# A first FFN block cut into two halves of 128 tokens, whose pieces are held back until their weights are rounded

## The chip, the core and the metric

The kernel runs on one core of a Trainium2 chip. Its engines work side by side, each through its own list of instructions in order: TensorE (PE in the profile, with its weight loads as PEld), VectorE (DVE), ScalarE (ACT), GpSimd (POOL) and SyncE (SP), which issues most of the DMAs. The metric is the device time of one execution in microseconds; the median of four runs of the kernel before is 1777.9 us (1777.15 to 1778.71).

## What is computed

```python
# attention: q, k, v of shape (8, 8, 576, 64)
scores = scale * np.matmul(q, k.transpose(0, 1, 3, 2))
kth = np.partition(scores, -32, axis=-1)[..., -32:-31]
scores = np.where(scores >= kth, scores, -1000000000.0)
attn = np.exp(scores - np.max(scores, axis=-1, keepdims=True))
attn = attn / (np.sum(attn, axis=-1, keepdims=True) + 1e-09)
o = np.matmul(attn, v)
# bridge: (B,H,S,D) -> (B*S, H*D), 4608 tokens of 512
x = o.transpose(0, 2, 1, 3).reshape(B * S, H * D)
# FFN: w_gate, w_val 512 x 1536, w_out 1536 x 512
g = x @ w_gate
out = (g * (1.0 / (1.0 + np.exp(-g))) * (x @ w_val)) @ w_out
```

## The kernel before

**Units.** Attention is cut into 160 units. A unit is one batch, one tile of 128 queries and one pair of heads; units run in the order batch, query tile, head pair, so four units make all 512 features of 128 tokens. The last query tile of each batch (`qt == J`, units 16 to 19 of the first batch) has 64 queries for both heads together and costs half. The main loop `for n in range(NU + 3)` (L747) writes for unit n, in this order: the scores of the units after it (`scores`, PE L306 or L292, scaled on ACT L311), the attention-times-v products of units n-4 and n-3 (`values`, PE L421, copied into `xT` on ACT L437), the exponentials of unit n-1 (`weigh`, ACT L353 and L358), the top-k of unit n (`select`, DVE L326 and L330), the transposes of unit n-2 (`turn`, PE L387), the normalizing of unit n-1 (`normalize`, DVE L369 and L370, then POOL L373). Scores and values are written in even units only, for two units at a time.

**FFN blocks.** The FFN takes 256 tokens at a time (`BLK`), 18 blocks. `feed(kb)` (L459 on) is a generator. For each of six steps s it multiplies the transposed tokens `xT` by two 128-column slices of `w_gate` and of `w_val` (PE L477, 128x256 moving), evacuates them with three ACT instructions for the gate (L502 to L504) and one for the value (L509), and multiplies on POOL (L505, L510) into a tile `h`. Then comes the product with `w_out`: twelve matmuls of 128x512 for each 128 tokens in block 0 (L523, the `plain` form), and seven quarter products (L563) in every later block. A `yield` ends a piece: in the first part four 128x256 matmuls, in the plain part two 128x512 matmuls. Each is one credit; three quarter matmuls are 0.75.

**Credit.** `share(n)` gives every unit a number of credits, 7 (later 6.4) less what its attention costs, and `pieces` spends them at four places of the unit. `piece()` starts the next block only when `done[kb]` says that all its tokens are in `xT`; without that it returns 0 and the credit is lost.

**Weights.** The three weight matrices are rounded on the chip while attention runs, in 36 pieces: `w_gate` and `w_val` in 24, in the order of the steps s, then twelve rows of `w_out`. Each piece is a DMA of 512 KB into one of three `w` buffers (L104), three ACT instructions (L112, L114, L115), one on DVE (L119) and two on POOL (L120, L121), the last of which frees the buffer. `rounding` and `early` place them among the instructions of the unit, some two and a half pieces in a unit; `ready[0]` counts those whose last step is written. In `feed`, `need(n)` writes roundings at once until n pieces are ready. After block 0, `weights` goes on to form sums of parts of `w_out` (L169 to L188) for the later blocks; a part of these waits for `plain_done`, which block 0 sets with its last product.

**Order.** Every engine keeps the order in which the code writes (the last loop of the function adds that dependency), so a waiting instruction holds what is written behind it on its engine.

Of the kernel before, what the change touches and what calls it, by code (L numbers as in the profile page):

```python
# [8 lines left out]
AF = mybir.ActivationFunctionType  # L9
ALU = mybir.AluOpType  # L10
FP32 = mybir.dt.float32
# [4 lines left out]
P = 128  # L16
# [4 lines left out]
BLK = 256  # L21
# [4 lines left out]
def kernel(  # L26
# [37 lines left out]
    nc = tc.nc  # L64
    B, H, S, D = q.shape
    DM, DFF = w_gate.shape
# [3 lines left out]
    NHP = H // 2  # L70
    KC = DM // P
    MC = DFF // P
    MS = MC // 2
    MQ = MC // 2
    NBLK = B * S // BLK
    scale = 1.0 / float(D) ** 0.5
# [8 lines left out]
    ffn = ctx.enter_context(tc.tile_pool(name="ffn", bufs=2))  # L85
    ps_t = ctx.enter_context(tc.tile_pool(name="ps_t", bufs=5, space=PSUM))
    ps_f = ctx.enter_context(tc.tile_pool(name="ps_f", bufs=3, space=PSUM))
# [9 lines left out]
    wg = consts.tile([P, KC, DFF], FP32, name="wg")  # L97
    wv = consts.tile([P, KC, DFF], FP32, name="wv")
    wo = consts.tile([P, MC, DM], FP32, name="wo")
# [93 lines left out]
    ready = [0]  # L193
    early = [lambda: None]
    plain_done = []
# [7 lines left out]
    def need(n):  # L203

        while ready[0] < n:
            next(weight)

    pairs = [(b, hp) for b in range(B) for hp in range(NHP)]
    raw, preps = {}, {}
# [186 lines left out]
    xT, done = {}, {}  # L396
# [47 lines left out]
    def store(o, g0, cols=slice(0, DM), queues=(nc.sync,)):  # L444

        at = g0
        while at < g0 + P:
            b, c = divmod(at, S)
            j, p0 = divmod(c, P)
            n = min(g0 + P - at, S - c, P - p0)  # L450
            r0 = b * S + (c if j == J else J * p0 + j)
            dst = out[r0 : r0 + n, :] if j == J else out[r0 : r0 + J * (n - 1) + 1 : J, :]
            queues[0].dma_start(dst[:, cols], o[at - g0 : at - g0 + n, cols])
            queues = queues[1:] + queues[:1]
            at += n

    on_act, on_pool = [], []

    def flush(queue):  # L459
        while queue:  # L460
            queue.pop(0)()

    def feed(kb):


# [2 lines left out]
        x = xT.pop(kb)  # L468
        hs = []

        def product(w, s, then):
            ps = ps_f.tile([P, 2, BLK], FP32, tag="f", name="f")
            need(4 * s + (2 if w is wg else 4))
            for i in range(2):
                m = 2 * s + i
                for kc in range(KC):
                    nc.tensor.matmul(  # L477
                        ps[:, i, :],
                        w[:, kc, m * P : (m + 1) * P],
                        x[:, kc, :],  # L480
                        start=(kc == 0),
                        stop=(kc == KC - 1),
                    )
                if i == 1:
                    on_act.append(lambda: then(ps))
                yield 1

        plain = kb == 0
        first, late = slice(0, P), slice(P, BLK)

        s32 = x[:].rearrange("p a b -> p (a b)")[:, 0 : MQ * P].rearrange(
# [3 lines left out]
        for s in range(MS):  # L495
            h = ffn.tile([P, 2, BLK], FP32, tag="h", name="h", bufs=MS + 1)
# [15 lines left out]
            yield from product(wg, s, gate)  # L512
            yield from product(wv, s, value)
        o = ffn.tile([P, 2, DM], FP32, tag="o", name="o", bufs=1)
        if plain:
            for t in range(2):
                ps = ps_f.tile([P, DM], FP32, tag="f", name="o_ps")
                for m in range(MC):
                    need(4 * MS + m + 1)
                    if m == 6:  # L520
                        flush(on_act)
                        flush(on_pool)
                    nc.tensor.matmul(  # L523
                        ps[:],
                        hs[m // 2][:, m % 2, t * P : (t + 1) * P],
                        wo[:, m, :],
                        start=(m == 0),
                        stop=(m == MC - 1),
                    )
                    if m == MC - 1:  # L530

                        def finish(ps=ps, t=t):
                            nc.scalar.copy(o[:, t, :], ps[:])
                            store(o[:, t, :], kb * BLK + t * P)

                        on_act.append(finish)
                        if t == 1:
                            plain_done.append(True)
                    if m % 2 == 1:
                        yield 1  # L540
            return
        while len(T[3]) < MQ:
            next(weight)
        DH = DM // 2
# [76 lines left out]
        if kb == NBLK - 1:  # L621
# [7 lines left out]
            for i, t, cols in ((4, 1, left), (3, 0, right)):  # L629
                ps = ps_f.tile([P, DH], FP32, tag="f", name="x_ps")  # L630
# [30 lines left out]
        on_act.append(rest_x)  # L661

    NU = len(units)
    todo = list(range(NBLK))
    current = []

    def piece():

        if len(on_act) > 1:
            flush(on_act)  # L670
        if len(on_pool) > 1:
            flush(on_pool)
        while True:
            if not current:
                if not todo or done.get(todo[0], 0) < NHP * BLK:
                    return 0
                flush(on_act)
                flush(on_pool)
                current.append(feed(todo.pop(0)))
            cost = next(current[0], 0)  # L680
            if cost == 0:
                current.pop()
                continue
            return cost
# [34 lines left out]
    def pieces(n):  # L719
        for _ in range(n):  # L720
            if credit[0] >= 1:
                credit[0] -= piece()
# [85 lines left out]
    while piece():  # L808
        pass
# [48 lines left out]
```

## Time and profile before

| | us |
|---|---|
| median of 4 runs | 1777.9 |
| profiled execution | 1779.02 |
| its span in the profile | 1777.2 |
| PE busy | 1679.6 (95%) |
| DVE busy | 1483.7 (83%) |
| ACT busy | 1163.4 (65%) |
| POOL busy | 959.3 (54%) |

The shares are means over stages that differ. Up to about 131 us the weights are rounded beside attention and no FFN block has begun; DVE works without a gap and PE is busy about half of the time. From there to the end PE is nearly always busy. DVE ends its last unit about 110 us before the end; what remains is FFN work of the last blocks. The start of a unit can be read on DVE: its first MAX8 reads `sc`, later ones read `e`. In the profile a fp32 matmul appears as two records of PE, so "x8" of L477 is four matmuls, one piece.

### The profile page before, as it was taken

Reading aid. Unit: us, or ns where it says so; the run is one execution under the profiler, and the core shown is the slowest. Engines: PE = TensorE matmul, PEld = TensorE weight load, DVE = VectorE, ACT = ScalarE, POOL = GpSimd, SP = SyncE. Lnnn points to the kernel's source line nnn. Section 1 sums busy time; section 2 is a strip of 40 time slices with the busy share of each in tenths; the row PEclk is TensorE's granted clock in tenths of the full one; section 3 lists DMA queues with packets and bytes.
Section 4 is the critical chain, followed back from the end, with each engine's and each line's share of the span. In section 5 each row is a group of like instructions: output and inputs, shape, how many; then the busy total and the mean of one; then the engine's idle time right before and its main releaser. Section 6 shows DMA issues by size and latency. Waiting matters only on the chain.

```text
span 1777.2 us, 31074 instructions
## 1 busy us (share of the span) xinstructions
PE 1679.6 (95%) x11012; PEld 1386.4 (78%) x11012; DVE 1483.7 (83%) x3371; ACT 1163.4 (65%) x2721; POOL 959.3 (54%) x1058
## 2 busy tenths in 40 slices
PE   5559999899999999999999999999999999999999
PEld 3337678688888878888888878887888878787887
DVE  6999888998999899998998888898988888888300
ACT  7788676676667576767666676666666666575521
POOL 3778655445464636464646445554445544646444
PEclk6669999899999999999999999999999999999999
DMA  7442030002100030002100020000300020000000
GB/s 194 129 119 84 21 87 1 13 1 62 35 5 9 15 82 2 13 1 51 47 13 1 13 71 26 1 13 17 80 1 13 1 56 14 13 1 13 1 13 12
DMA packets 109307, 59.68 MB, mean 34 GB/s; under 512 B 88544, under 2 KB 96992, under 8 KB 109152
## 3 DMA queue, kind: packets, MB, share of 16 engines
q1 hardware_dynamic: 108016, 57.37, 12.4%
q8 instruction: 87, 1.43, 0.3%
q14 instruction: 68, 0.56, 0.1%
q10 hardware_dynamic: 1136, 0.33, 0.1%
HBM read 48.23 MB, written 9.44 MB: 32 GB/s over the span
## 4 chain that ended last, share of the span: by engine, by line
PE 78%; POOL 8%; ACT 6%; DVE 4%; issue 3%; DMA 1%; SPq 0%; POOLq 0%; ACTq 0%; DVEq 0%
PE f L477 38%; PE av L421 10%; PE x_ps L563 8%; PE s L306 7%; PE etps L387 6%; PE y_ps L563 6%; POOL e L373 2%; ACT e L358 2%; DVE e L330 2%; DVE m L326 2%; PE s L292 2%; PE kqps L261 1%; PE o_ps L523 1%; ACT e L353 1%; POOL size L120 1%
## 5 line engine op out<-in xcount | busy, mean ns | idle before, releaser
L326 DVE MAX8 m<-e 128x8 f32<-128x576 f32 x864 | 615.5, 749 | 3.3
L330 DVE MATCH_REPLACE8 e<-m,e 128x576 f32<-128x576 f32 x576 | 424.1, 743 | 0.0
L477 PE MATMUL f<-xT,wg 128*128 128x256 f32 x1728 | 401.2, 381 | 0.0
L477 PE MATMUL f<-xT,wv 128*128 128x256 f32 x1728 | 399.7, 380 | 0.3 <-ACT half_g L503 0.3
L373 POOL TENSOR_TENSOR e<-e,tot 128x576 f32<-128x576 f32 x288 | 325.0, 1147 | 120.9 <-DVE tot L370 106.5
L477 PEld LDWEIGHTS f<-xT,wg 128*128 128x128 f32 x1728 | 323.3, 190 | 50.5 <-issue 8.5
L477 PEld LDWEIGHTS f<-xT,wv 128*128 128x128 f32 x1728 | 322.9, 190 | 49.7 <-issue 7.9
L505 POOL TENSOR_TENSOR h<-h,half_g 128x512 f32<-128x512 f32 x108 | 137.8, 1276 | 294.9 <-ACT h L504 291.6
L358 ACT ACTIVATE e<-e,bias 128x576 f32<-128x576 f32 x288 | 220.4, 768 | 75.6 <-POOL bias L341 73.2
L510 POOL TENSOR_TENSOR h<-h,val 128x512 f32<-128x512 f32 x108 | 137.7, 1275 | 184.8 <-ACT val L509 161.9
L387 PE MATMUL etps<-ident,e 128*128 128x128 f32 (+1 forms) x1312 | 184.3, 282 | 49.7 <-POOL e L373 29.2
L387 PEld LDWEIGHTS etps<-ident,e 128*128 128x128 f32 (+1 forms) x1312 | 154.4, 143 | 83.9 <-POOL e L373 39.2
L353 ACT ACTIVATE e<-sc,m 128x576 f32<-128x576 f32 x288 | 210.3, 778 | 7.6 <-DVE m L326 7.3
L330 DVE MATCH_REPLACE8 e<-m,sc 128x576 f32<-128x576 f32 x288 | 211.9, 743 | 0.0
L326 DVE MAX8 m<-sc 128x8 f32<-128x576 f32 x288 | 203.4, 743 | 9.2 <-ACT sc L311 9.2
L311 ACT ACTIVATE sc<-s 128x288 f32<-128x288 f32 x512 | 167.3, 414 | 62.4 <-PE s L306 61.9
L306 PE MATMUL s<-kqT 64*128 64x288 f32 x1024 | 174.1, 453 | 30.3 <-ACT et L388 17.9
L369 DVE TENSOR_SCALAR tot<-tot 128x1 f32<-128x1 f32 x288 | 36.5, 145 | 198.6 <-ACT e L358 198.5
L388 ACT COPY et<-etps 128x512 f32<-128x512 f32 (+1 forms) x448 | 182.6, 485 | 26.1 <-PE etps L387 26.1
L421 PE MATMUL av<-et,v 128*64 128x128 f32 (+1 forms) x2560 | 162.2, 271 | 0.0
L306 PEld LDWEIGHTS s<-kqT 64*128 64x128 f32 x1024 | 95.3, 195 | 78.6 <-issue 26.4
L421 PEld LDWEIGHTS av<-et,v 128*64 128x64 f32 x2560 | 140.5, 142 | 7.0 <-issue 3.6
(71 smaller groups left out, 1908.8 us busy)
## 6 DMA issues: line engine op xcount, KB each, us to landing
v<-in_v_dram SPq DMA_DIRECT2D x32, 256.0 KB, 3.2
kq_in<-in_k_dram SPq DMA_DIRECT2D x63, 128.0 KB, 2.9
kq_in<-in_q_dram SPq DMA_DIRECT2D x63, 128.0 KB, 3.2
w<-in_moe_w_gate_dram SPq DMA_DIRECT2D x12, 512.0 KB, 3.7
w<-in_moe_w_val_dram SPq DMA_DIRECT2D x12, 512.0 KB, 3.7
w<-in_moe_w_out_dram SPq DMA_DIRECT2D x12, 512.0 KB, 3.7
out_dram<-o SPq DMA_DIRECT2D x38, 128.0 KB, 2.4
out_dram<-o SPq DMA_DIRECT2D x16, 256.0 KB, 2.4
```

The source lines that it names most:

```text
L306: nc.tensor.matmul(ps[:, 0:half], slab[d, q0 : q0 + P], slab[d, k0 : k0 + half])
L311: nc.scalar.mul(sc[:, i * half : (i + 1) * half], ps[:, 0:half], scale)
L326: nc.vector.max(m[:, t, 8 * r : 8 * r + 8], cur[:, hs])
L330: nc.vector.match_replace(e[:, hs], m[:, t, 8 * r : 8 * r + 8], cur[:, hs], LOWEST)
L353: nc.scalar.activation(e[:, hs], sc[:, hs], AF.Prelu, bias=m[:, t, TOP_K - 1 : TOP_K], scale=-1.0, alpha=SMALL,)
L358: nc.scalar.activation(e[:, hs], e[:, hs], AF.Exp, bias=bias[:, t : t + 1], scale=-1.0 / SMALL, accum_out=tot[:, t : t + 1],)
L373: nc.gpsimd.tensor_tensor(e[:, hs], e[:, hs], tot[:, t : t + 1].to_broadcast([P, S]), ALU.mult)
L387: nc.tensor.transpose(ps[0:kl, c * P : (c + 1) * P], e[:, k0 : k0 + kl], ident[:])
L388: nc.scalar.copy(et[0:kl, c0 : c0 + cn, :], ps[0:kl, 0 : cn * P].rearrange("p (c j) -> p c j", c=cn),)
L421: nc.tensor.matmul(av[d, i, 0:ql], weights_, moving, start=c == (0 if last else J), stop=c == (J if last else J - 1),)
L477: nc.tensor.matmul(ps[:, i, :], w[:, kc, m * P : (m + 1) * P], x[:, kc, :], start=(kc == 0), stop=(kc == KC - 1),)
L563: nc.tensor.matmul(ps, lhsT, T[i][m], start=m == 0, stop=m == MQ - 1)
```

## The change

Block 0 is no longer fed by `feed(0)` but by `feed_half(0)` and `feed_half(1)`, each for 128 of its tokens. `piece()` starts the first half as soon as query tile 0 is in `xT` (128 tokens, four head pairs), the second half when tile 1 is. A half has three groups of four 128-column slices; the moving side is 128x128, a PSUM tile holds four slices, and an evacuation covers [128, 4, 128], the same 128x512 as before. A piece is two slices, eight matmuls. Instead of `need`, a half asks `sure(n)`: whether two roundings more than the n it uses are written. If not, it yields `None`, `piece()` returns 0, the credit stays, and the next place in the unit asks again. The `plain` branch of `feed` goes away; block 1 and later are as before.

```diff
+    def sure(n):
+
+        return ready[0] >= min(n + 2, 4 * MS + MC)
...
+    def feed_half(t):
+
+        x = xT[0]
+        cols = slice(t * P, (t + 1) * P)
+        hs = []
+
+        def product(w, g, then):
+            ps = ps_f.tile([P, 4, P], FP32, tag="f", name="f")
+            for i in range(4):
+                m = 4 * g + i
+                while not sure(4 * (m // 2) + (2 if w is wg else 4)):
+                    yield None
+                for kc in range(KC):
+                    nc.tensor.matmul(
+                        ps[:, i, :],
+                        w[:, kc, m * P : (m + 1) * P],
+                        x[:, kc, cols],
+                        start=(kc == 0),
+                        stop=(kc == KC - 1),
+                    )
+                if i == 3:
+                    on_act.append(lambda: then(ps))
+                if i % 2 == 1:
+                    yield 1
+
+        for g in range(MC // 4):
+            h = ffn.tile([P, 4, P], FP32, tag="h", name="h", bufs=MS + 1)
...
+            yield from product(wg, g, gate)
+            yield from product(wv, g, value)
+        if t == 1:
+            xT.pop(0)
+        o = ffn.tile([P, 2, DM], FP32, tag="o", name="o", bufs=1)
+        ps = ps_f.tile([P, DM], FP32, tag="f", name="o_ps")
+        for m in range(MC):
+            while not sure(4 * MS + m + 1):
+                yield None
...
+            nc.tensor.matmul(
+                ps[:], hs[m // 4][:, m % 4, :], wo[:, m, :], start=(m == 0), stop=(m == MC - 1)
+            )
...
-        plain = kb == 0
...
-        if plain:
-            for t in range(2):
...
-                    need(4 * MS + m + 1)
...
-            return
...
-    todo = list(range(NBLK))
+    todo = [(0, 0), (0, 1)] + [(kb, None) for kb in range(1, NBLK)]
...
-                if not todo or done.get(todo[0], 0) < NHP * BLK:
+                if not todo:
+                    return 0
+                kb, t = todo[0]
+                if done.get(kb, 0) < NHP * (P if t == 0 else BLK):
                     return 0
                 flush(on_act)
                 flush(on_pool)
-                current.append(feed(todo.pop(0)))
+                todo.pop(0)
+                current.append(feed(kb) if t is None else feed_half(t))
             cost = next(current[0], 0)
+            if cost is None:
+                return 0
```

More of the change, by code (lines that the diff above doesn't have):

```diff
@@ L461, in flush, with gate, value, finish @@
             queue.pop(0)()
+    def feed_half(t):
[22 more added lines that the diff above has]
+            h = ffn.tile([P, 4, P], FP32, tag="h", name="h", bufs=MS + 1)
+            hs.append(h)
+            def gate(ps, h=h):
+                half = ffn.tile([P, 4, P], FP32, tag="gv", name="half_g", bufs=3)
+                nc.scalar.activation(h[:], ps[:], AF.Tanh, scale=0.5)
+                nc.scalar.mul(half[:], ps[:], 0.5)
+                nc.scalar.add(h[:], h[:], 1.0)
+                on_pool.append(lambda: nc.gpsimd.tensor_mul(h[:], h[:], half[:]))
+            def value(ps, h=h):
+                val = ffn.tile([P, 4, P], FP32, tag="gv", name="val", bufs=3)
+                nc.scalar.copy(val[:], ps[:])
+                on_pool.append(lambda: nc.gpsimd.tensor_mul(h[:], h[:], val[:]))
+            yield from product(wg, g, gate)
[7 more added lines that the diff above has]
+                yield None
+            if m == 6:
+                flush(on_act)
+                flush(on_pool)
+            nc.tensor.matmul(
+                ps[:], hs[m // 4][:, m % 4, :], wo[:, m, :], start=(m == 0), stop=(m == MC - 1)
+            )
+            if m == MC - 1:
+                def finish(ps=ps):
+                    nc.scalar.copy(o[:, t, :], ps[:])
+                    store(o[:, t, :], t * P)
+                on_act.append(finish)
+                if t == 1:
+                    plain_done.append(True)
+            if m % 2 == 1:
+                yield 1
@@ L514, in feed @@
         o = ffn.tile([P, 2, DM], FP32, tag="o", name="o", bufs=1)
-        if plain:
-            for t in range(2):
-                ps = ps_f.tile([P, DM], FP32, tag="f", name="o_ps")
-                for m in range(MC):
-                    need(4 * MS + m + 1)
[L520 to L540, printed above, removed]
-            return
         while len(T[3]) < MQ:
```

## The prediction, made before the changed kernel was run

> **What bounds the kernel now.** I read the busy time by stage first.
>
> ```profile
> core 0: us, PE busy (x) PEld busy (x) DVE busy (x) ACT busy (x) POOL busy (x), PEclk, DMA share, GB/s
> 75.00:131.00 56.00, 30.45 (x194) 21.58 (x194) 55.54 (x127) 47.50 (x103) 44.97 (x40) 0.62 0.41 115
> 131.00:186.00 55.00, 52.84 (x328) 43.37 (x326) 51.92 (x107) 49.12 (x107) 47.41 (x42) 1.00 0.29 85
> 207.00:327.00 120.00, 116.61 (x819) 91.92 (x817) 100.39 (x230) 79.20 (x193) 64.39 (x71) 1.00 0.15 36
> 327.00:345.00 18.00, 12.17 (x79) 8.61 (x78) 17.93 (x43) 10.86 (x29) 4.63 (x5) 0.72 0.08 31
> 345.00:700.00 355.00, 351.95 (x2387) 295.86 (x2386) 322.03 (x737) 243.10 (x578) 183.66 (x211) 1.00 0.11 26
> ```
>
> Up to 131 us DVE binds and PE has room; from 131 to 327 PE binds; from 327 to 345 DVE binds once more, because FFN has run out of tokens; after that PE to the end. The waits of DVE and the PE timeline show how the stages are tied.
>
> ```profile
> DVE tot L369 <- ACT e L358: 22.3, 15, 6.4
> ...
> 91.50 0.86 PE L387 MATMUL etps<-ident,e 128*128 128x128 f32 x5 [3.50 <-ACT sc L311]
> ...
> 186.47 1.99 PE L477 MATMUL f<-xT,wg 128*128 128x256 f32 x8
> ...
> 207.46 1.19 PE L292 MATMUL s<-kqT 64*64 64x288 f32 x8
> ...
> 265.72 1.15 PE L387 MATMUL etps<-ident,e 128*128 128x128 f32 x9
> 266.70 1.89 PE L477 MATMUL f<-xT,wg 128*128 128x256 f32 x8
> ...
> 333.78 2.43 PE L387 MATMUL etps<-ident,e 128*128 128x128 f32 x9 [3.26 <-POOL e L373]
> ```
>
> DVE's only wait from 80 to 345 us is for the exponentials, 22.3 us in all, mostly where PE is late with scores (6.4 us ahead of 213.5, when the scores at 207.46 came late). At 333.78 it is PE that waits. Last, four timelines side by side at unit 7:
>
> ```profile
> 92.56 1.29 POOL L121 TENSOR_TENSOR wg<-size,w 128x512 f32<-128x512 f32 x1
> ...
> 90.96 1.29 ACT L311 ACTIVATE sc<-s 128x288 f32<-128x288 f32 x4
> ...
> 97.71 0.67 ACT L112 ACTIVATE size<-w 128x512 f32<-128x512 f32 x1 [0.84 <-DMA w<-in_moe_w_val_dram]
> ...
> 102.17 0.18 ACT L358 ACTIVATION_READ_ACCUMULATOR e<-e,bias 128x1 f32 x1
> ...
> 103.04 0.20 DVE L369 TENSOR_SCALAR tot<-tot 128x1 f32<-128x1 f32 x2
> ```
>
> POOL frees a weight buffer at 93.8; the transfer lands and ACT rounds at 97.7; the exponentials stand behind that and end at 102.35, 0.7 us before DVE wants them. So in the rounding stage the loop POOL, DMA, ACT is within 0.7 us of stopping DVE, though ACT and POOL are busy only 80 to 85%.
>
> **What the Trainium skill says.** "TensorE: Matmul & The Clock Gate", LDWEIGHTS, has a weight load take its columns over 1.2 GHz, 107 ns for 128, whatever the moving side is. Here nine 128x128 transposes, each with such a load, take 0.98 us (265.72 to 266.70), 109 ns each, so a record of 128 moving columns just covers its load. A 256-column piece runs at 1.73 us for eight records, 216 ns. The same page's HAM section has the clock at half after an idle window of some 3.4 us; the trace agrees (PEclk 0.62 while PE has gaps, 1.00 from 131). "PSUM — Partial Sum Buffer", Engine vs sequencer instructions, calls the queues of ScalarE, VectorE and GpSimd strict FIFO: the lines at unit 7 show it on ACT.
>
> **What moves.** The built order of both kernels gives the credits spent in each unit. DVE's order is the same instruction for instruction, and PE's is identical from unit 28 on, by when both have spent 70.5. So only the arrival at unit 28 can differ, and everything later shifts with it. Units 6 to 13: before 0 0 0 0 4 7 3 7 (21), after 4 5 0 2 1 2 1 1 (16): the halves wait for their weights. Units 14, 15: 3, 7 against 4, 7. Units 16 to 21 alike, four pieces behind; one is made up in unit 22, the last three in unit 27. A piece costs 1.73 us before; after, 16 records of 109, 1.74. Evacuations and POOL products are as many and as wide as before (12 gate and value groups in all), so PE, ACT and POOL gain or lose no work, only places. On SP the DMAs stay in order up to the first store of block 0; the second store moves behind the batch-1 loads of the next units (it stood ahead of them at 231.89, held back for ACT's copy), which frees those loads rather than holding them; they are wanted some units later, so I cost it at nothing.
>
> **Step A, units 6 to 13.** DVE's unit starts before are 94.14 (unit 7), 106.12, 116.75, 128.72 (unit 10), 139.34, 155.41, 168.03, 181.77 (unit 14). A pair of undisturbed units takes 11.98 + 10.62 = 22.6, so without stalls unit 14 would start at 128.72 + 45.2 = 173.9; before lost 7.9 us there. After takes fewer pieces in units 10 to 13 and avoids these, but puts three groups of evacuations into units 6 to 12, in the tight loop. In POOL's order the first gate product stands ahead of the third rounding of its unit. Its gate is ready after the score copies at 92.1 and three ACT instructions of 0.6, at 93.9; product 1.3 and rounding 2.7 bring the buffer's release to 97.9 for 93.8; transfer 3.9, ACT 1.7, exponentials 3.1: 106.6, where DVE is ready at 103.04: a stall of 3.5. Following the second gate and both values through the same queues gives 1.2 in unit 8 and 2.5 in unit 9; the third group comes where ACT and POOL have 1.7 and 2.2 us idle and costs up to 0.5. That is 7.7; some of it may be absorbed by those idle times, and I take 6.5, with 0 and 9 as ends. PE is no limit: nine pieces (15.7 us) and 6.3 of attention fit in 22.6, and unbroken they keep its clock at full. Unit 14 starts at 180.4, 1.4 before the old time, with five pieces less done.
>
> **Step B, units 14 and 15.** PE finishes the even unit's scores and values 3.7 us after DVE starts it (132.38 to 128.72): 184.1. There the first half still waits for `w_out` rows, so its pieces come behind the transposes, five of which wait for a bank (3.50 at unit 6). Transposes 1.1 and that wait: 188.7. Then 11 pieces (19.0) and the next transposes (1.0): PE reaches unit 16's scores at 208.7, for 207.46: 1.2 late, four pieces owing.
>
> **Step C, units 16 to 26.** PE binds, so the piece of unit 22 costs 1.7. Evacuations of the second half fall here in place of plain products; PE waits for one of those 0.3 before, and 0.5 to 0.9 for POOL around the quarter products; I add 1.0 (0 to 3). 192 records at 109 for half of 216 add 0.2. Late by 4.1.
>
> **Step D, unit 27.** Three pieces more, 5.2, fall where FFN is short of tokens. Before, the exponentials of unit 27 end at 329.2 and DVE wants them at 332.02: 2.8 of cover. So 2.4 remains, and DVE is 4.1 + 2.4 = 6.5 late from there. The 5.6 us that PE sat idle at 327 to 338 is not a gain beyond that, since there PE waits for DVE's unit.
>
> **Sum.** Span 1777.2 + 6.5 = 1783.7; the profiled execution is 1779.0, the median 1777.9, so 1784 on the median's scale. The ends: no stall in A and nothing added in C gives unit 14 at 173.9, 5.3 early at unit 16, 3.5 early at unit 26 and, with 2.4 from D, 1.1 early: 1777. Stalls of 9 and 3 in C give 11 late: 1789.
>
> **Rivals.** (1) No change: the stalls of A come to 2 to 3, since one late buffer is caught up in POOL's 2.2 us of idle time per unit; the result is then 1 to 3 late, 1779 to 1781. For it: both engines have room on average. Against: only 0.7 us of cover in each unit. (2) Faster: A has no stall, as PE's pieces lie in DVE-bound time, and the cover at units 27 to 29 takes the whole debt. Then the 3.5 early at unit 26 stays: 1774.4. It decides only if unit 14 starts by 174 and the exponentials of unit 27 come no later than DVE's want. For it: 63 us of PE's idle time before 140. Against: 0.7. (3) Much slower: 128-column records don't cover their loads. Fully in the open, 192 records of the second half at 107 add 20 (1804); the transposes at 109 speak against it, a tenth of it is 2. (4) The halves don't fill PE's room because `sure` holds them: that is already in the counts, 16 pieces for 21.
>
> **Numbers.** Forecast (3.6 to 11 late) 0.56; no change 0.25; faster 0.11; weight loads or a worse loop (over 11) 0.08. A change under about 0.2% (3.6 us) can't be told from none in a measurement of this kernel. So faster 0.11, same 0.25, slower 0.64. The range runs from 1775, at the edge of the faster case, to 1792, into the fourth.
>
> **What would show it.** Right: DVE waits for ACT L358 in units 7 to 9 (none over 0.3 before) with ACT's first rounding instruction waiting for a weight transfer; DVE starts unit 14 at 178 to 183; the plain product of the second half ends after 235 (231 before); a wait of DVE in unit 27 or 28; from unit 30 a constant shift. Wrong: unit 14 at 174 to 176, or PE reaching unit 28 before 322 us, or records of 128 columns further apart than 115 ns in the second half.

## The result, and the profile after

The changed kernel takes 1782.6 us (median of 31 runs, 1780.7 to 1784.7), the kernel before beside it 1779.5 (49 runs): a ratio of 1.0018, with a 95% interval of 1.0012 to 1.0023. Its profiled execution took 1781.5 us with a span of 1779.7, for 1779.02 and 1777.2 before. The time forecast was 1784.0, but the way there was not the one forecast: 6.1 us more than the kernel before was forecast, and 3.1 more was measured. Two readings show how: the stages, and the waits.

The busy time by stage of the changed kernel, with the columns as in the prediction:

```profile
core 0: us, PE busy (x) PEld busy (x) DVE busy (x) ACT busy (x) POOL busy (x), PEclk, DMA share, GB/s
75.00:131.00 56.00, 42.35 (x338) 36.42 (x336) 52.86 (x119) 48.08 (x104) 46.71 (x41) 0.83 0.36 104
131.00:186.00 55.00, 38.24 (x243) 24.67 (x239) 54.17 (x120) 48.39 (x107) 44.45 (x41) 0.84 0.33 97
207.00:327.00 120.00, 118.00 (x811) 94.65 (x808) 101.56 (x232) 78.92 (x190) 66.36 (x72) 1.00 0.14 34
327.00:345.00 18.00, 14.71 (x129) 11.07 (x126) 16.89 (x40) 12.10 (x33) 5.01 (x7) 0.91 0.08 31
```

PE is busy for 12 us more before 131 us and for 15 us less from 131 to 186. DVE, which had hardly a gap up to 131, now idles for 3.1 of 56 us there, and for 1.1 us from 327 to 345. From 207 to 327 PE still binds, with 118.0 busy for 116.6. The waits of DVE between 80 and 345 us (line waited for: total, times, longest) give the same in one line:

```profile
DVE tot L373 <- ACT e L362: 25.4, 17, 7.8
```

It is the same wait as before, for the exponentials, and it has grown from 22.3 to 25.4 us. 3.0 of that lie in unit 7, where before there was nothing over 0.3.

One profile of each kernel isn't enough to add up a difference this small: at unit 42 (452.80 and 452.71 us) the two first profiles don't differ at all, though the times do. The experiments gave three more profiles of each kernel that are the same up to the last unit. The start of units on DVE, as means of four profiles each:

| unit | 8 | 10 | 14 | 16 | 20 | 26 | 28 | 29 | 42 | 159 |
|---|---|---|---|---|---|---|---|---|---|---|
| before, us | 105.8 | 128.4 | 180.9 | 202.2 | 232.7 | 300.7 | 324.35 | 334.3 | 452.1 | 1682.85 |
| after, us | 108.8 | 132.4 | 178.7 | 199.5 | 233.6 | 303.3 | 324.35 | 335.5 | 453.6 | 1684.4 |
| after less before | +3.0 | +4.0 | -2.1 | -2.7 | +0.9 | +2.6 | 0.0 | +1.2 | +1.5 | +1.5 |

The single profiles spread: unit 42 lies between 450.9 and 452.8 us in the kernel before and between 452.7 and 455.1 in the changed one. So the last differences are not clear of the noise by themselves, and the times in the next section have to support them. The change loses 4 us up to unit 10, gains 6 up to unit 14, where five pieces are left out and the kernel before lost 7.9 us, and then gives everything back: 3.6 in the four half units 16 to 19, 1.7 for the piece of unit 22, and, after a gain of 2.6 in units 26 and 27, 1.2 in unit 28. From unit 42 the difference is 1.5 us, to the last unit.

### The profile page after: what moved, and what is told of

The parts are those of the page before. It is cut to its first block, busy times and chain, and to the rows that moved or that the text cites. A ratio compares the mean times of both kernels' runs of the same rounds, so it can differ in the third digit from the quotient of the medians.

```text
span 1779.7 us, 31455 instructions
## 1 busy us (share of the span) xinstructions
PE 1680.9 (94%) x11204; PEld 1394.7 (78%) x11204; DVE 1481.2 (83%) x3371; ACT 1162.7 (65%) x2721; POOL 959.6 (54%) x1058
## 3 DMA queue, kind: packets, MB, share of 16 engines
q8 instruction: 89, 1.46, 0.4%
## 4 chain that ended last, share of the span: by engine, by line
PE 79%; DVE 7%; ACT 6%; POOL 4%; issue 3%; DMA 1%; SPq 0%; POOLq 0%; ACTq 0%; DVEq 0%
PE f L549 38%; PE av L425 9%; PE x_ps L607 8%; PE s L310 7%; PE y_ps L607 6%; PE etps L391 6%; DVE m L330 3%; DVE e L334 3%; ACT e L362 2%; POOL e L377 2%; PE s L296 1%; PE kqps L265 1%; ACT e L357 1%; PE f L480 1%; PE o_ps L520 1%
## 5 line engine op out<-in xcount | busy, mean ns | idle before, releaser
L549 PE MATMUL f<-xT,wg 128*128 128x256 f32 x1632 | 379.7, 382 | 0.0
L549 PE MATMUL f<-xT,wv 128*128 128x256 f32 x1632 | 377.4, 380 | 0.0
L549 PEld LDWEIGHTS f<-xT,wg 128*128 128x128 f32 x1632 | 306.6, 191 | 47.2 <-issue 6.9
L549 PEld LDWEIGHTS f<-xT,wv 128*128 128x128 f32 x1632 | 305.0, 190 | 46.7 <-issue 7.9
L576 POOL TENSOR_TENSOR h<-h,half_g 128x512 f32<-128x512 f32 x102 | 130.0, 1274 | 288.3 <-ACT h L575 288.1
L581 POOL TENSOR_TENSOR h<-h,val 128x512 f32<-128x512 f32 x102 | 130.1, 1276 | 184.8 <-ACT val L580 167.8
L334 DVE MATCH_REPLACE8 e<-m,sc 128x576 f32<-128x576 f32 x288 | 211.9, 743 | 0.0
```

Of the source, the lines that this page charges most:

```text
L334: nc.vector.match_replace(e[:, hs], m[:, t, 8 * r : 8 * r + 8], cur[:, hs], LOWEST)
L549: nc.tensor.matmul(ps[:, i, :], w[:, kc, m * P : (m + 1) * P], x[:, kc, :], start=(kc == 0), stop=(kc == KC - 1),)
```

## The experiments

The theories, in the order in which they are named below. P (path): the difference arises in the first 345 us and every later unit keeps it. C (clock): it arises at the end, where PE waits 2.98 us ahead of the last transposes and its clock falls. A: a late weight buffer stalls DVE in units 7 and 8, since POOL makes the gate and value products first. L: any lead is lost in units 16 to 19.

**The end of the kernel.** The changed kernel once more (no edit), both kernels with six matmuls that nothing reads put into PE's gap at the end, the pair of these once more, and one more profile of the kernel before.

```diff
+        if n - TURN == NU - 1:
+            warm = ps_t.tile([P, 512], FP32, tag="t", name="warm")
+            for _ in range(6):
+                nc.tensor.matmul(warm[:, 0:256], ident[:], wg[:, 0, 0:256])
```

The changed kernel again:

> The changed kernel once more, for a second profile of it. Theory P (path): the 3 us of the median come from the first 340 us, and the first profile, whose unit 42 starts 0.1 us before the old one, was a lucky execution; here unit 42 then starts 2 to 4 us after the old 452.8. Theory C (clock): unit 42 starts within 0.5 us of 452.8 again, and what the span is longer by lies behind 1705 us, where PE waits 3 us for POOL and its clock falls to half for one window (before) or three (after). Ratio 1.0012 to 1.0023 under both.

The kernel before with the filler:

> The old kernel with six matmuls of 128x256 (2.6 us at full clock) whose result nobody reads, put into the 3 us gap of PE ahead of the last transposes. Nothing else differs. Theory C: the clock stays full there, the first FFN piece behind it takes 3.6 us for 4.6, and the median falls by 1.5 to 3 us. Theory P has nothing to say on this gap: 0 to -1.6 (the 1.0 and 0.6 us that the old profile lost at half clock).

The changed kernel with the filler:

> The changed kernel with the same six matmuls. Theory C: the difference between the two kernels was the clock, so this one comes out within 0.5 us of the old kernel with the filler. Theory P: it stays 3 us behind the old kernel with the filler, and the start of unit 42 lies 2 to 4 us behind the old one's.

The same two once more:

> The kernel before with the six unread matmuls ahead of the last turn, timed again beside the changed kernel with the same. Path theory: with the clock's fall at the end taken away in both, what is left of the difference is the first 345 us, and it stays at 1.3 us (means of 1776.7 and 1778.0 before). If the whole difference of 2.8 us between the two kernels lies at the end (clock theory alone), both have the same mean within 0.4 us; if it is all path, they are 2.4 or more apart.

> The changed kernel with the same six matmuls. Path theory: a mean of 1778.0, 1.3 us above the kernel before with them; clock theory alone: 1776.7; all path: 1779.1 or more.

The kernel before once more:

> The kernel before once more, for its unit starts alone. Where the clock falls differently in each execution (theory C), unit 42 starts at 450.9 (as in its run with the filler) or at 452.8 (as in the profile before), and the tenth to twelfth units differ by up to 2 us between executions, with the same waits of DVE otherwise; without that, unit 42 is at 452.8 within 0.3.

Measured: the changed kernel 1781.6 us (ratio to the kernel before beside it, at 1778.6, 1.0017, 1.0010 to 1.0023); before with filler 1776.6 and 1776.9 (0.9985, 0.9978 to 0.9991, and 0.9989, 0.9981 to 0.9997); the changed kernel with filler 1777.6 and 1779.0 (0.9994, 0.9986 to 1.0002, and 0.9998, 0.9989 to 1.0006). The PE timeline of the changed kernel at the end (start, duration, line, operation, in brackets the idle time before and what ended it):

```profile
1705.86 0.77 PE L391 MATMUL etps<-ident,e 128*128 128x128 f32 x5
1709.60 1.33 PE L391 MATMUL etps<-ident,e 128*128 128x128 f32 x5 [2.98 <-POOL e L377]
...
1713.78 6.00 PE L549 MATMUL f<-xT,wg 128*128 128x256 f32 x16
```

and of the kernel before with the filler:

```profile
1704.66 2.76 PE L798 MATMUL warm<-wg,ident 128*128 128x256 f32 x12
1707.80 0.77 PE L387 MATMUL etps<-ident,e 128*128 128x128 f32 x5 [0.39 <-POOL e L373]
...
1710.25 3.72 PE L477 MATMUL f<-xT,wg 128*128 128x256 f32 x16
```

After the gap of 2.98 us the same sixteen records take 6.00 us and the transposes 1.33; with the gap filled they take 3.72 and 0.77. The gap is there in the kernel before too (2.98 at 1709.66 us). From the start of unit 159 to the end it takes 92.3 us in each of the six profiles with the filler (four in this section, two under "Together"). In the eight without, the half clock lasts 3.4, 6.8 or 10.2 us, and the same stretch takes 93.7 us in the one profile with 3.4, 95.2 and 95.4 in the two with 6.8, and 96.2 to 96.5 in the five with 10.2. So the fall of the clock costs 1.5, some 3 or some 4 us, and the filler takes all of it away.

Taken over all runs of the experiments, the filler lowers the mean of the kernel before by 2.4 us (95% interval 2.0 to 2.8) and that of the changed kernel, from its run here, by 3.4 (2.7 to 4.1). What is left between the two with the filler is 1.7 us (1.2 to 2.2; 26 and 34 runs; 1.3 and 2.0 in the two pairs), of a whole difference of 2.8 (2.2 to 3.5) in the runs of this section, or 3.1 (2.7 to 3.5) over all runs. So neither P nor C alone holds: 1.7 is path, which agrees with the 1.5 of the table of units, and 1.1 to 1.4 belongs to the end. Why the end should cost the changed kernel more isn't settled. The clock's fall lasted 3.4 us in one profile of the kernel before and 10.2 in the other, so it is no fixed property of either kernel, and in the runs of this section the interval of the excess nearly reaches zero.

The second profile of the kernel before had unit 42 at 452.67, as in the first profile; with the filler, which comes 1250 us later, it is at 450.9 and 452.1. In the changed kernel it is at 452.71, 455.05, 452.75 and 454.00, so no single profile decides between P and C. Unit 12 starts at 155.4, 154.7, 153.7 and 154.4 in the four profiles of this kernel. Executions of one kernel differ by some 2 us on the path too.

**Step A, the products of POOL.** The first half's products are put behind the roundings and the normalizing that are written for the same unit.

```diff
-                on_pool.append(lambda: nc.gpsimd.tensor_mul(h[:], h[:], half[:]))
+                (late_pool if t == 0 else on_pool).append(lambda: nc.gpsimd.tensor_mul(h[:], h[:], half[:]))
...
+        flush(late_pool)
```

> The changed kernel with the POOL products of the first half moved behind the roundings and the normalizing of their unit, so that no rounding stands behind a gate. Theory of step A: the stall of 3.0 us in unit 7 falls to under 1.2 and unit 14 starts 2 to 3 us earlier (176 to 177 for 178.9). For the end: if the path up to unit 14 decides (P), the median falls by 2 to 3 us; rival L: the lead is lost in units 16 to 19 as in the first profile, where 3.8 us of lead at unit 16 were 0.1 at unit 20, and the median moves by less than 0.7 us.

Measured: 1777.9 us (0.9996, 0.9988 to 1.0004), a mean 3.4 us below the changed kernel's (2.5 to 4.2). Unit 8 starts at 105.92, unit 14 at 175.1, and unit 29 at 331.50 for 335.32. The changed kernel in unit 7, timelines of POOL, ACT and DVE:

```profile
93.15 1.29 POOL L501 TENSOR_TENSOR h<-h,half_g 128x512 f32<-128x512 f32 x1 [1.72 <-ACT h L500]
94.40 1.29 POOL L120 TENSOR_TENSOR size<-size,w 128x512 int32<-128x512 int32 x1
95.77 1.30 POOL L121 TENSOR_TENSOR wg<-size,w 128x512 f32<-128x512 f32 x1
...
101.20 0.69 ACT L112 ACTIVATE size<-w 128x512 f32<-128x512 f32 x1 [3.10 <-POOL h L506]
...
105.15 0.15 DVE L373 TENSOR_SCALAR tot<-tot 128x1 f32<-128x1 f32 x1 [2.36 <-ACT e L362]
105.91 0.15 DVE L373 TENSOR_SCALAR tot<-tot 128x1 f32<-128x1 f32 x1 [0.61 <-ACT e L362]
```

With the products behind:

```profile
92.73 1.31 POOL L121 TENSOR_TENSOR wg<-size,w 128x512 f32<-128x512 f32 x1
93.98 2.26 POOL L377 TENSOR_TENSOR e<-e,tot 128x576 f32<-128x576 f32 x2
96.19 1.31 POOL L501 TENSOR_TENSOR h<-h,half_g 128x512 f32<-128x512 f32 x1
...
98.07 0.69 ACT L112 ACTIVATE size<-w 128x512 f32<-128x512 f32 x1
...
102.83 0.20 DVE L373 TENSOR_SCALAR tot<-tot 128x1 f32<-128x1 f32 x2
```

Read these as one chain. The rounding that frees the weight buffer ends at 97.07 for 94.04, 3.0 us later: 1.29 for the gate product ahead of it and 1.72 that POOL waits for ACT to make the gate. ACT's first rounding instruction follows 4.1 us behind that end in the one and 4.0 in the other; a transfer into such a buffer takes 3.6 to 4.0 us from issue to landing, by the page's medians (the page names POOL L506 as the releaser, but that isn't an input of L112; an instruction that waits for several things is put down to the one that came last in the records). And 2.36 + 0.61 = 2.97 us is what DVE waits. Another 0.5 us of lead comes in unit 8, where a rounding instruction of DVE takes 0.93 us for 1.46. All of it reaches the end of the path: A and P hold, with a little more than A's 2 to 3 us. L, under which the lead would be lost again, falls: 3.8 us at unit 16 are 3.8 at unit 29.

**Holding the pieces.** Here they are not held but ask for their weights, as block 0 did before.

```diff
-                while not sure(4 * (m // 2) + (2 if w is wg else 4)):
-                    yield None
+                need(4 * (m // 2) + (2 if w is wg else 4))
...
-            while not sure(4 * MS + m + 1):
-                yield None
+            need(4 * MS + m + 1)
```

> The two halves stay, but their pieces no longer hold for rounded weights: like the block before, a piece asks for its weights, so 36 pieces instead of 16 are issued by the end of unit 13 and all weights are asked for by unit 10 instead of unit 15. Theory A (the loop of POOL, DMA and ACT is what a unit in the rounding stage has least of): 14 rounded pieces instead of 7 in units 8 to 10 put some 19 us more of POOL's work into three units that have 2.2 us of room each, so DVE stalls over 8 us there and unit 14 starts at 186 or later (178.9 in the changed kernel). Units 14 to 18 then run without FFN pieces at DVE's pace (22.3 us for 14 and 15), 9 pieces fewer lie from unit 16 to 28, worth up to 15.6: the time is between 4 us faster and 8 us slower than the changed kernel, and the lead at unit 28 is unit 14's delay + 2 - 15.6. Rival H (holding the pieces only puts them off): unit 14 starts at 176 to 180 and the time is over 8 us below the changed kernel, about 1772.

Measured: 1809.1 us (1.0175, 1.0162 to 1.0189), 27.5 above the changed kernel. The delay is the one that A expected (unit 14 starts at 223.2, where A had 186 or later), but the time is beyond both ends of its range. The waits of DVE from 80 to 190 us, and a piece in PE's timeline:

```profile
DVE size L119 <- ACT size L112: 32.2, 11, 13.0
...
116.28 1.22 PE L479 MATMUL f<-xT,wg 128*128 128x128 f32 x4 [10.75 <-POOL wg L121]
```

The expectation counted POOL's work alone. What was missing is PE's order: a piece written behind roundings that haven't run holds PE for 10.75 us, and the scores and values behind it with it; ACT's score copies wait for these, the next roundings stand behind the copies on ACT, and DVE, which now has rounding instructions early in its own queue, waits up to 13.0 us for them. Unit 9 starts at 149.8 us for 120.6. So in this kernel halves without the hold are far worse than whole blocks, and the hold is what makes the cut bearable.

**The rows of w_out.** PE waits 7.6 us for the rounding of `w_out` in three places between 131 and 188 us, which the prediction had not foreseen. Here these pieces hold for four further roundings instead of two.

```diff
-    def sure(n):
+    def sure(n, more=2):

-        return ready[0] >= min(n + 2, 4 * MS + MC)
+        return ready[0] >= min(n + more, 4 * MS + MC)
...
-            while not sure(4 * MS + m + 1):
+            while not sure(4 * MS + m + 1, 4):
```

> For the rows of w_out the pieces hold until four further roundings have been issued instead of two. Theory W (in units 14 and 15 PE waits 7.6 us for POOL's rounding of w_out because a piece is issued two roundings behind): these waits fall below 2 us, one piece moves from units 11 to 13 to unit 28, and unit 16 starts no later than before (199.3), up to 1.7 us earlier; unit 28 then gets 0.75 of a piece, 1.3 us, uncovered. Path theory: the sum is 1 us faster to 1.5 us slower than the changed kernel. Rival (the waits lie beside work that DVE needs anyway): they go and unit 16 starts at the same time within 0.3; then 1 to 2 us slower.

Measured: 1778.5 us (0.9997, 0.9988 to 1.0005), a mean 3.5 us below the changed kernel's (2.6 to 4.4), more than either side expected. The three waits fall from 7.6 us to one of 0.8, in unit 14 at 187.0 us, and unit 16 starts at 199.16 for 199.25: in that the rival is right, the waits lay beside work that DVE needed. The gain comes later: unit 17 at 211.9 for 213.7, unit 19 at 224.0 for 227.6.

**Units 16 to 18.** No FFN pieces at all in these units:

```diff
+        if hold[0]:
+            return 0
...
+        hold[0] = 16 <= n <= 18
```

> No FFN piece in units 16 to 18, so the evacuations of the second half no longer stand before the exponentials there; the three pieces go later, the last into unit 28. Theory L (the evacuations lose the lead of 3.8 us in units 16 to 19): the waits of DVE for exponentials of 0.77 and 1.25 us in units 17 and 18 go, unit 19 starts at 223.5 to 225.5 instead of 227.6, and of this lead 5.2 us is paid back for three pieces in units 21 to 28, with up to 0.6 more of DVE's wait in unit 28: 1.5 us slower to 1 us faster than the changed kernel. Rival (three pieces are simply shifted and the evacuations cost nothing): unit 19 is only as much earlier as the lead over the old kernel was at unit 16 (223.8), and the time is the changed kernel's plus 2 to 4 us, since unit 28 has no cover for pieces.

Measured: 1781.0 us (1.0008, 1.0002 to 1.0015), a mean 1.3 us below the changed kernel's (0.3 to 2.2). Unit 19 starts at 225.45 and unit 29 at 334.65 for 335.32. L's expectation in its narrow form (evacuations ahead of the exponentials cost some of the lead in these units) holds, at the fast edge of its range; the rival's 2 to 4 us slower doesn't.

Both runs point at the same instructions. The changed kernel in units 16 to 18, timelines of ACT, POOL and DVE:

```profile
212.40 0.60 ACT L498 ACTIVATE h<-f 128x512 f32<-128x512 f32 x1
...
217.74 0.78 ACT L362 ACTIVATE e<-e,bias 128x576 f32<-128x576 f32 x1 [1.94 <-POOL bias L345]
218.42 0.19 ACT L362 ACTIVATION_READ_ACCUMULATOR e<-e,bias 128x1 f32 x1
218.51 0.56 ACT L505 COPY val<-f 128x512 f32<-128x512 f32 x1
...
214.08 1.27 POOL L501 TENSOR_TENSOR h<-h,half_g 128x512 f32<-128x512 f32 x1 [8.43 <-ACT h L500]
215.31 2.25 POOL L377 TENSOR_TENSOR e<-e,tot 128x576 f32<-128x576 f32 x2
217.51 0.19 POOL L345 TENSOR_TENSOR bias<-m 128x1 f32<-128x1 f32 x1
...
218.64 0.15 DVE L373 TENSOR_SCALAR tot<-tot 128x1 f32<-128x1 f32 x1 [0.77 <-ACT e L362]
...
225.81 0.15 DVE L373 TENSOR_SCALAR tot<-tot 128x1 f32<-128x1 f32 x1 [1.25 <-ACT e L362]
```

With the longer hold for `w_out`, one piece fewer has been done by unit 16, and the groups end one unit later:

```profile
210.67 2.25 POOL L377 TENSOR_TENSOR e<-e,tot 128x576 f32<-128x576 f32 x2 [5.19 <-DVE tot L374]
212.88 0.19 POOL L345 TENSOR_TENSOR bias<-m 128x1 f32<-128x1 f32 x1
215.54 1.28 POOL L501 TENSOR_TENSOR h<-h,half_g 128x512 f32<-128x512 f32 x1 [2.47 <-ACT h L500]
```

It is the pattern of step A once more. The gate product stands ahead of the normalizing and of `bias` on POOL, and the exponentials of ACT wait 1.94 us for `bias`; DVE waits for those. With the product behind `bias`, units 17 and 18 take 5.8 and 6.2 us, for 6.7 and 7.2. Another 1.7 us come from unit 16, whose scores PE reaches at 203.32 for 205.12, because one piece fewer stands ahead of them. For the wait of 1.25 us in unit 18 the timeline shows only that the value's copy (218.51) and product come shortly before it; it is 0.29 us with the longer hold, where that copy is moved, and gone where no piece stands in units 16 to 18. No finer cause was looked for.

**Together.** First the products behind with the filler, then these and the longer hold:

> The first half's gate and value products on POOL are put behind the roundings, as in the earlier run of that edit, and six unread matmuls of 256 columns stand ahead of the last turn, as in the two runs with filler. Path and clock add: the mean was 3.4 us lower with the first alone and 3.8 with the second alone, so 7 us below the changed kernel's 1781.8: 1774.6, and 4 below the kernel before. If both took away the same cost (the clock's fall at the end comes only with a late arrival): 1777.5 to 1778.

> Three edits together: the first half's products on POOL behind the roundings, a hold of four roundings for the w_out rows, and the unread matmuls ahead of the last turn. Alone they lowered the mean of the changed kernel by 3.4, 3.5 and 3.8 us. If the first two take away different losses (the stall in units 7 and 8; the delay of exponentials in units 16 to 18) they add: unit 14 starts at 174.5, unit 17 no more than 12.8 after unit 16, unit 42 at 446 to 447, and the mean is 1771 to 1772. If both only shift one and the same wait: 1774.6, as with the first and the third.

Measured: 1775.2 us (0.9978, 0.9970 to 0.9986) and 1771.6 us (0.9955, 0.9941 to 0.9968), with means of 1774.6 and 1771.3. The edits add, as expected; unit 14 of the second starts at 174.9, unit 17 comes 13.3 behind unit 16 (12.8 was the bound), and unit 42 starts at 446.9. It is 7.3 us faster than the kernel before and the best of all. Only five runs of it were made, within 1.3 us of each other. Against the mean of the kernel before with the same filler, 5.4 us remain (4.8 to 5.9). That is what halves are worth together with a hold long enough for `w_out` and products that stay out of the way. Neither another place for the products nor a hold was tried in the kernel before, so how much of the 5.4 the cut into halves gives by itself isn't known.

## Why the prediction was right or wrong

**What moves: right.** All that the change does to the time of attention has happened by unit 28 or 29. The difference is 1.2 us at unit 30 and 1.5 at unit 159.

**Step A: the chain right, but it struck once.** The chain POOL, DMA, ACT, DVE is the one forecast, and the stall in unit 7 was 3.0 us for 3.5. Then the late buffer was caught up: from 106 to 140 us DVE waits for nothing. Unit 8 is 1.0 us longer than an undisturbed one, for 1.2 forecast, but that agreement is luck. What is longer is a rounding instruction of DVE itself, in the changed kernel:

```profile
113.76 1.46 DVE L119 TENSOR_SCALAR size<-size 128x512 int32<-128x512 int32 x1
```

and in the kernel before, in unit 8 and in unit 12:

```profile
110.94 0.42 DVE L119 TENSOR_SCALAR size<-size 128x512 int32<-128x512 int32 x1
...
162.86 1.51 DVE L119 TENSOR_SCALAR size<-size 128x512 int32<-128x512 int32 x1
```

The 2.5 of unit 9 did not come. Unit 10 is 0.9 longer, of which 0.6 is a wait for the exponentials that stays with the products behind. Unit 14 started at 178.9 (178 to 183 was the range), 5.0 behind the undisturbed 173.9, for 6.5. Nor did PE's clock stay full, as the step had it: the mean is 0.83 up to 131 us and 0.84 from there to 186.

The step was right that the changed kernel avoids most of the 7.9 us that the kernel before lost in units 11 to 13. But the same instruction made up most of them: six of the eight instructions of L119 there take 1.3 to 1.5 us, for two in undisturbed units, which is 4.5 us more in all, while the waits for the exponentials come to 2.8. In the two first profiles the long ones lie beside instructions of POOL for all but 0.3 us of their time at most. But two short ones lie wholly beside POOL too, and no run separates the cause.

**Step B: wrong, by 3.6 us.** It had the first half's pieces behind transposes that wait 3.5 us for a bank of PSUM, and eleven pieces after 188.7. PE in the changed kernel:

```profile
182.80 1.88 PE L520 MATMUL o_ps<-wo,h 128*128 128x512 f32 x4
187.00 1.12 PE L520 MATMUL o_ps<-wo,h 128*128 128x512 f32 x2 [2.32 <-POOL wo L121]
187.97 3.73 PE L480 MATMUL f<-xT,wg 128*128 128x128 f32 x32
...
205.12 1.19 PE L296 MATMUL s<-kqT 64*64 64x288 f32 x8
```

There was no wait for a bank but one for `w_out`; the last pieces of the first half ran before it and around it, and only nine pieces remained after 187.97: 0.7 + 2.9 us less than forecast. So PE reached unit 16's scores at 205.12 where 208.7 was forecast: 2.3 ahead of the kernel before, not 1.2 behind.

**Step C: the place right, one term too small.** The piece of unit 22 cost 1.7 us as forecast. The evacuations in units 16 to 19 were put at 1.0 (0 to 3): of PE's lead of 2.3 us at unit 16's scores all but 0.1 was gone at unit 20 in the first profiles, so they cost 2.2. The reason isn't that PE waits for evacuations, as the step had it, but the POOL and ACT order shown above. "0.2 for 192 records at 109" held: the 32 records from 187.97 to 191.54 are 112 ns apart.

**Step D: the mechanism right, its other half missing.** The waits of DVE in unit 28, from its timeline, are the ones forecast:

```profile
331.52 0.15 DVE L373 TENSOR_SCALAR tot<-tot 128x1 f32<-128x1 f32 x1 [0.44 <-ACT e L362]
332.28 0.15 DVE L373 TENSOR_SCALAR tot<-tot 128x1 f32<-128x1 f32 x1 [0.60 <-ACT e L362]
```

They come to 1.04 us, where 2.4 was forecast. Three pieces put PE's scores for unit 28 at 325.34 for 322.31: 3.0 late, where 5.2 on top of the 4.1 of step C was forecast. Two waits of PE for POOL, 0.88 and 0.45 us at 319 and 320 us in the kernel before, are gone. And PE wasn't late when it came to these pieces: in the kernel before it waits 0.54 and 0.88 us for POOL ahead of the scores of unit 26, in the quarter products, and DVE there waits 2.33 for the exponentials. In the changed kernel these quarter products come three pieces later, behind those scores, which are 0.4 us earlier than before; the lateness of DVE in unit 26 (2.6 us in the means) is made good by unit 28. The prediction costed the pieces and not the waits that moved with them.

**The sum.** 6.5 us late was forecast, 1.5 to 1.7 is what the path shows. The remaining 1.1 to 1.4 us of the measured 2.8 to 3.1 are in no term of the sum: they lie at the end, in the clock. So 1784.0 for 1782.6 is partly luck, in two ways. The sum started from the 1777.9 us of four runs, and the kernel before took 1779.5 in the 49 beside the changed one: that alone brings the forecast 1.6 us nearer. And the clock at the end, which the prediction didn't name, added 1.1 to 1.4 us where the path lost some 5 us less than forecast.

**The rivals.** The first rival comes nearest. The path's loss has its size (1 to 3 late), and half of its reason held: one late buffer cost 3.0 us and was caught up. But A's delays came to 5.0 us in all, not 2 to 3, and the pieces left out before unit 14 outweighed them; the loss of the path arose in units 16 to 28. The second, faster, fell as it said itself that it would: unit 14 came at 178.9, not by 174. It shows what was there to be had, though: with the products out of the way and the longer hold, unit 14 at 174.9 and unit 17 soon after, a gain appeared. The third fell with the 112 ns. The fourth was in the counts; the run without the hold shows that filling the room costs 27.5 us.

**What would show it.** The waits for ACT's exponentials were in unit 7, not in units 8 and 9; unit 14 within its range; the second half's plain product ended after 235 (its last copy is at 245.9); the wait in unit 28 came; the shift is constant from unit 42; from unit 30 to there it grows by 0.3 us, for which no cause was looked for.

## What to carry to other kernels

On an engine with a queue in order, look at what stands behind an instruction that is moved in, and who waits for that: a product of 1.3 us ahead of a buffer's release, or of a one-column `bias`, cost more than its own length, because the product also waited for its own input there: 3.0 us of DVE's time in the first case, and in the second a wait of 1.94 us for ACT. Put such work behind what frees buffers and what feeds the next engine, and hold a matmul back until its operands are sure, since a matmul that waits holds everything written after it. A difference of 0.2% can't be located in the span of one profile: it takes the starts of units, averaged over several profiles, and many timed runs beside them.

## What the hardware showed that was not expected

The clock of PE changes only at points of a grid of 3413 ns in the clock records of all fourteen traces, and the place of this grid against the kernel's start differs in each execution. The Trainium skill, "TensorE: Matmul & The Clock Gate", What's actually happening, says so too (a free-running window of 4096 cycles, 3413 ns). But it gives the throttled state after at least one idle window of some 3.4 us, and full speed after at least one busy window. Here a gap of 2.98 us was enough: in the first profile of the changed kernel the fall is recorded at 1708.2 us, 1.6 us after the gap began, so the window before it wasn't idle throughout. The half clock then lasted one to three windows (3.4, 6.8 or 10.2 us), though PE was busy again from the end of the gap. In all eight profiles with the gap the clock fell there, and in none of the six with the filler. Six matmuls of 256 columns, which cost nothing as they lie in the gap, saved 2.4 us of the kernel before.
